# A fused backward kernel: tiles 4 and 5 of the opening each with a square root of its own and a place of its own on TensorE, tile 1 turned two products later

## The chip, the cores and the metric

The kernel runs on one core of one Trainium2 chip. The metric is the time of one execution on the device in microseconds (us). Lower is better. All times below are of one core; "TensorE" multiplies matrices, "VectorE" and "ScalarE" work on elements, "GpSimd" (POOL) and "SyncE" (SP) mostly issue transfers.

## The reference

The reference computes a forward pass and the gradients of nine of its inputs. `x` is `A_q`, 2048 rows of 1024 (bf16).

```python
def _layernorm(x, axis=-1, eps=1e-5):
    m = jnp.mean(x, axis=axis, keepdims=True)
    v = jnp.var(x, axis=axis, keepdims=True)
    return (x - m) / jnp.sqrt(v + eps)
...
    def _B_ref(x, W_gate, W_up, W_down):
        gate = jnp.einsum("bsd,df->bsf", x, W_gate)
        up = jnp.einsum("bsd,df->bsf", x, W_up)
        gate = gate * (lambda x, dt: x.astype(dt))(gate > 0, gate.dtype)
        h = gate * up
        return jnp.einsum("bsf,fd->bsd", h, W_down)
    x = A_q
    xn = _layernorm(x, axis=-1)
    return x + _A_ref(xn, A_k, A_v, A_shift_k, A_ssm_k, A_ssm_D) + _B_ref(xn, B_W_gate, B_W_up, B_W_down)
...
    _out, _vjp = jax.vjp(_f, A_q, A_k, A_v, A_shift_k, A_ssm_k, A_ssm_D, B_W_gate, B_W_up, B_W_down)
    _grads = _vjp(grad_out)
```

`_A_ref` is a long convolution along the rows, done with Fourier transforms; `_B_ref` is a gated layer with 3584 hidden columns. What the change touches is the layer norm of the first six tiles of 128 rows and the first products with `W_gate`, `W_up` and `W_down`.

## The kernel before

The 2048 rows are 16 tiles of 128. The program has a first phase (`hidden`, L1188) that computes the layer norm, gate, up and the gradient of the hidden layer; then the weight gradients (`ps_d`, `ps_w`), the output and the gradient of `x`. `hidden` goes through 14 stages: two halves of 8 tiles, and in each half seven blocks of 512 hidden columns. In a stage each tile has three rows of work on TensorE, each of eight products of 128x128 by 128x512: a gate row (`ps_g`, with `wg`), an up row (`ps_u`, with `wu`) and a gradient row (`ps_h`, from the turned gradient `goT` and the turned `W_down`, `wdT`). The convolution's work is interleaved from later stages on.

Stage 0 is the opening: nothing is there yet, and the layer norm, the loads and the products run against each other. The order on TensorE is written out by hand (`keep_in_program_order`), and so is most of that on VectorE and ScalarE.

- `ln_load` (L941) loads tiles 0 to 3 one by one, tiles 4 and 5 as one chunk in two transfers (the second one is `ln_rest`, L955), and then chunks of two tiles (`LN_CHUNKS`). Chunk 5 holds tiles 6 and 7.
- `layer_norm` (L958) is a generator; each `next(ln)` issues the next part. For a tile it takes the mean (on ScalarE a pass that sums, `sums`, L968; on VectorE `bn_stats`), subtracts it (`moved`, L1008), takes the sum of squares on ScalarE, then a root: `variance` (L1011) and `root` (L982) add epsilon on VectorE and take the square root on ScalarE, `inverse` (L987) refines and inverts it on VectorE. Tiles 0 to 2 are turned and multiplied with the mean off but unscaled (`bare`), and scaled later by `rstd`; from tile 3 on a tile is scaled (`scale`, L997) before it is turned. `kept` (L1029) scales a copy of tiles 0 to 2 for the store of `xn`.
- `flip_xn` (L1152) turns a tile on TensorE: eight 128x128 products with the identity into a PSUM bank (`pst_x`), then copies into `xnT` on VectorE (on ScalarE for tile 4). Tiles 6 and 7 are turned by DMA.
- `first_rows` (L1278) is the order of the first rows: gate rows of tiles 0 and 1 pair by pair of products, up rows likewise, then gate and up of tiles 2 and 3, with functions called in the middle (`second_tile`, `third_tile`, `last_mid`). `flip(k)` turns all tiles below `k` that aren't turned. In `up`, `mid` is called after four products, `after={k: f}` behind product k, counted from 0.
- `grad` (L1417) does gradient rows in pairs; in row 1 it calls `flip_ahead` (L1388) after four products, which turns tiles 4 and 5 one after the other. Then `gate_up(4)` does gate rows 4 and 5, up rows 4 and 5; `grad(2)` and `grad(4)` follow with gradient rows 2 to 5.
- Before anything else `warm` (L1173) issues 40 products of zeros, 128 wide, while the first tile is loaded.
- Products of a stage store `h` and `ug` through POOL's queue; loads go through SP's queue, in the order in which they are issued there.

The wait for a value is on the engine's own queue: each engine works through its instructions in order, and one that waits holds those behind it.

Of the kernel before, what the change touches and what calls it, by code (L numbers as in the profile page):

```python
# [14 lines left out]
ALU = mybir.AluOpType  # L15
# [864 lines left out]
class LnMlp:  # L880
# [77 lines left out]
    def layer_norm(self, xn_d, jpool, jtag, spool):  # L958
# [5 lines left out]
        def act(out, in_, func, **kw):  # L964
            self.ln_act = nc.scalar.activation(out=out, in_=in_, func=func, **kw)
            return self.ln_act

        def sums(out, x, func, **kw):  # L968
            jk = jpool.tile([P, D], BF16, name="ln_j", tag=jtag)
            return act(jk[:, 0:x.shape[-1]], x, func, accum_out=out, **kw)  # L970
# [50 lines left out]
        def half_mean(x, s, b, k):  # L1021
            part = spool.tile([P, 2, 6], F32, name="ln_bn")
            hold(V.bn_stats(out=part[:, 0], in_=x[:, 0:h]))
            hold(sums(s[:, 0, k:k + 1], x[:, h:D], ACT.Copy, scale=-1.0 / D))
            hold(V.tensor_tensor(out=s[:, 1, k:k + 1], in0=part[:, 0, 1:2], in1=part[:, 0, 4:5], op=ALU.add))
            hold(V.scalar_tensor_tensor(out=b[:, 0, k:k + 1], in0=s[:, 1, k:k + 1], scalar=-0.25, in1=s[:, 0, k:k + 1],
                                        op0=ALU.mult, op1=ALU.add))

        def kept(out, c, st):  # L1029
            hold(V.tensor_scalar(out=out, in0=c, scalar1=self.rstd[:, st:st + 1], scalar2=None, op0=ALU.mult))  # L1030
            self.kept.append(lambda: nc.gpsimd.dma_start(out=xn_d[st * P:(st + 1) * P, :], in_=out))
# [19 lines left out]
            hold(V.bn_stats(out=bn[:, k], in_=x2[:, k * h:k * h + h]))  # L1051
        hold(V.bn_aggr(out=b2[:, 0:2, 0], in_=bn[:].rearrange("p h s -> p (h s)")))
        hold(moved(c2, x2, b2[:, 0, 0:1], ALU.subtract))
        half_mean(x3, s2, b2, 1)
        hold(sums(s2[:, 2, 1:2], x3, ACT.Square, bias=b2[:, 0, 1:2]))
        self.xn.append(c2)
        yield
        self.pri.now()
        kept(n0, c0, 0)
        hold(V.tensor_scalar(out=b2[:, 1, 1:2], in0=s2[:, 2, 1:2], scalar1=1.0 / D, scalar2=None, op0=ALU.mult))  # L1060
        root(s2, b2, 2, hold)
        hold(moved(x3, x3, b2[:, 0, 1:2]))
# [1 line left out]
        hold(scale(x3, 3))  # L1064
        done(x3, 3)
        yield
        kept(n1, c1, 1)
        kept(n2, c2, 2)
        yield
        st0 = 4  # L1070
        for i, n in list(enumerate(self.LN_CHUNKS))[4:]:
            xt = self.ln_x[i]
            self.pri.now()
            sm, smb = small()
            if i == 4:
                for j in range(n):
                    hold(sums(sm[:, 0, j:j + 1], xt[:, j, :], ACT.Copy, scale=-1.0 / D))
                    hold(act(smb[:, 0, j:j + 1], sm[:, 0, j:j + 1], ACT.Copy))
                    hold(sums(sm[:, 2, j:j + 1], xt[:, j, :], ACT.Square, bias=smb[:, 0, j:j + 1]))
                    moved(xt[:, n + j, :], xt[:, j, :], smb[:, 0, j:j + 1])  # L1080
                    yield
            else:
                for j in range(n):
                    ins = sums(sm[:, 0, j:j + 1], xt[:, j, :], ACT.Copy)
                    if j == 0:
                        hold(ins)
                V.tensor_scalar(out=smb[:, 0, 0:n], in0=sm[:, 0, 0:n], scalar1=-1.0 / D, scalar2=None, op0=ALU.mult)
                for j in range(n):
                    sums(sm[:, 2, j:j + 1], xt[:, j, :], ACT.Square, bias=smb[:, 0, j:j + 1])
                    moved(xt[:, n + j, :], xt[:, j, :], smb[:, 0, j:j + 1])  # L1090
                yield
            variance(sm, smb, n, free)
            root(sm, smb, n, free)
            yield
            inverse(sm, smb, n, st0, free)
            self.pri.now()
            for j in range(n):
                scale(xt[:, n + j, :], st0 + j)
                done(xt[:, n + j, :], st0 + j)
            st0 += n  # L1100
            yield
# [50 lines left out]
    def flip_xn(self, st):  # L1152
        xT = self.act_tile("xnT", st)
        if st > 5:
            self.turned = self.nc.sync.dma_start_transpose(out=xT[:].rearrange("p (a b) -> p a b", b=P),
                                                           in_=self.xn[st])
            return xT
        k1 = 0
        for h in {0: (2, 2, 4), 1: (4, 4)}.get(st, (8,)):
            k0, k1 = k1, k1 + h  # L1160
            pst = self.ps.tile([P, self.DT, P], BF16, name="pst_x", tag="bps")
            for kt in range(k0, k0 + h):
                self.pri.pin(self.nc.tensor.transpose(pst[:, kt, :], self.xn[st][:, kt * P:(kt + 1) * P],
                                                      self.ident[:]), always=True)
            c = 4 if st in (2, 3) else h
            for k in range(k0, k0 + h, c):
                copy = self.nc.scalar.copy if st == 4 else self.nc.vector.tensor_copy
                self.copied = copy(out=xT[:, k * P:(k + c) * P], in_=pst[:, k:k + c, :].rearrange("p a b -> p (a b)"))
                if st < 5:
                    self.tc.keep_in_program_order(self.copied)  # L1170
        return xT
# [16 lines left out]
    def hidden(self, first, goT, load, ln, tables, Wg, Wu, Wd, g, xn_d, h_d, ug_d):  # L1188
# [6 lines left out]
        for n in range(N):  # L1195
# [82 lines left out]
            def first_rows():  # L1278

                held = []  # L1280

                def pair(name, w, seq, after):
                    banks = [self.ps_tile(name) for _ in range(2)]
                    for i, (s, q) in enumerate(seq):
                        for kt in (2 * q, 2 * q + 1):
                            self.pri.pin(nc.tensor.matmul(banks[s][:], lhsT=xT[s][:, kt * P:(kt + 1) * P], rhs=w(kt),
                                                          start=(kt == 0), stop=(kt == self.DT - 1)), always=True)
                        if i in after:
                            after[i]()
                    return banks  # L1290

                def second_tile():
                    flip(2)
                    next(ln)

                def third_tile():
                    flip(3)
                    next(ln)
                    flag(0)
                    flag(1)  # L1300

                def last_mid():
                    flip(4)
                    for f in held:
                        f()
                    next(ln)
                    chunk(1)
                ps = pair("ps_g", wg, ((0, 0), (0, 1), (0, 2), (1, 0), (1, 1), (1, 2), (0, 3), (1, 3)), {0: second_tile})
                for s in range(2):
                    gate(s, True, ps=ps[s])  # L1310
                    yield from step()
                next(ln)
                ps = pair("ps_u", wu, [(s, q) for q in range(4) for s in range(2)], {5: third_tile})
                for s in range(2):
                    up(s, None, {}, lambda *fs: held.extend(fs), True, ps[s])
                    yield from step()
                gate(2, True)
                yield from step()
                up(2, None, {3: last_mid})
                chunk(1)  # L1320
                yield from step()
                gate(3, True)
                chunk(1)
                yield from step()
                up(3, hold=True)
                chunk(1)
                yield from step()

            def gate_up(sp):
                end = sp == HS - 2  # L1330
                if ahead:
                    flip(sp + 2)
                for s in (sp, sp + 1):
                    gate(s)
                    yield from step(self.PACE[0])
                if end:
                    (load_up if ahead else load_gate)()
                for s in (sp, sp + 1):
                    up(s)
                    yield from step(self.PACE[1])  # L1340
                if end and ahead:
                    for q in range(4):
                        load_down(q)
                elif end:
                    load_up()
                if swap:
                    next_rows(sp)
# [38 lines left out]
                    next_grads(sp + 2)  # L1386

            def flip_ahead(sp):  # L1388
                flip(min(sp + 6, HS))
                if sp == 0:  # L1390
                    with self.tc.issue_after(self.copied.ins):
                        chunk()

# [33 lines left out]
                        next(ln)  # L1427

            if ahead:
                self.warm(40)  # L1430
                next(ln)
                flip(1)
                next(ln)
                yield from first_rows()
# [516 lines left out]
```

## Time and profile before

| what | us |
|---|---|
| runs of the kernel | 1857.24, 1853.23, 1857.38 |
| their median | 1857.24 |
| the profiled execution, its own time | 1854.18 |
| its span in the profile | 1852.0 |
| TensorE busy in the span | 1843.9 |
| VectorE, ScalarE busy | 1119.3, 646.3 |

The profile is of one execution. PE is TensorE's products, PEld its weight loads, DVE VectorE, ACT ScalarE, POOL GpSimd, SP SyncE; a "q" behind the name means the sequencer of that engine, which issues transfers. A row of a timeline has the start in us from the start of the span, the length, engine, line of the source, operation, what it writes and reads, how many of them, and in brackets how long the engine had been idle and what ended that. Successive instructions of an engine can overlap in such rows, since a row ends when the last result is written. L10xx and L11xx are lines of the kernel before; in the changed kernel the same code stands nine lines further down in the layer norm's last part and in `flip_xn`, and nine to seventeen further in `hidden`.

### The profile page before, as it was taken

How to read it: one execution, taken by the hardware profiler on the slowest of the kernel's cores; microseconds unless marked ns; L12 is line 12 of the kernel's file. 1: busy time of each engine (PE TensorE's matmuls, PEld its weight loads, DVE VectorE, ACT ScalarE, POOL GpSimd, SP SyncE). 2: the span in 40 equal slices, each digit the busy share in tenths (PEclk: the TensorE clock that was granted, in tenths of full speed). 3: DMA queues.
4: the chain of work that ended last, by engine and by line, in shares of the span. 5: the costliest groups of instructions: out<-in, count | busy, mean ns of one | idle time of the engine just before them, and what ended most of it. 6: DMA issues, size and time to landing. Idle time of an engine off the chain costs nothing.

```text
span 1852.0 us, 32391 instructions
## 1 busy us (share of the span) xinstructions
PE 1843.9 (100%) x13184; PEld 848.3 (46%) x13184; DVE 1119.3 (60%) x1651; ACT 646.3 (35%) x1212; POOL 34.9 (2%) x72
## 2 busy tenths in 40 slices
PE   9999999999999999999999999999999999999999
PEld 4444444444444444444444444444444544444444
DVE  6656798698789758485685677821212222566652
ACT  5644544444454454545544554330000000111100
POOL 1200000000000000000000000000000000000000
PEclk9999999999999999999999999999999999999999
DMA  9996669968767866639567445379999867799973
GB/s 240 285 241 168 154 163 233 218 172 199 186 158 193 250 156 169 160 105 270 136 149 179 140 119 158 108 229 248 261 232 255 182 145 170 172 210 216 204 152 74
DMA packets 746822, 345.18 MB, mean 186 GB/s; under 512 B 578105, under 2 KB 715313, under 8 KB 746673
## 3 DMA queue, kind: packets, MB, share of 16 engines
q1 hardware_dynamic: 732880, 311.39, 70.7%
q10 hardware_dynamic: 9632, 17.04, 3.0%
q0 software_dynamic: 4160, 14.68, 2.4%
q8 instruction: 103, 1.69, 0.4%
q14 instruction: 47, 0.38, 0.1%
HBM read 143.79 MB, written 103.83 MB: 134 GB/s over the span
## 4 chain that ended last, share of the span: by engine, by line
PE 96%; DVE 1%; SPq 1%; DMA 1%; issue 0%; ACT 0%; DVEq 0%
PE ps_x L1800 21%; PE ps_w L1503 20%; PE ps_o L1668 10%; PE ps_g L1119 10%; PE ps_u L1119 10%; PE ps_h L1119 10%; PE ps_d L1503 9%; PE ps_c L83 4%; PE ps_d L1519 2%; SPq L1137 0%; PE ps_r L1702 0%; PE ps_w L1519 0%; DMA xn_nat<-xn_d 0%; DVE arena L343 0%; DMA wg<-in_B_W_gate_dram 0%
## 5 line engine op out<-in xcount | busy, mean ns | idle before, releaser
L1503 PE MATMUL ps_w<-ugs,xn_nat 128*128 128x512 bf16 x1728 | 381.1, 379 | 0.0
L87 ACT CAST arena<-ps_c 128x512 bf16<-128x512 f32 x576 | 293.8, 611 | 104.1 <-PE ps_c L83 103.9
L1119 PEld LDWEIGHTS <-xnT 128*128 128x128 bf16 x1760 | 169.1, 98 | 204.8 <-issue 5.0
L1503 PEld LDWEIGHTS <-xn_nat 128*128 128x128 bf16 x1728 | 165.4, 98 | 200.7 <-issue 6.1
L343 DVE STREAM_TRANSPOSE arena<-arena 128x1024 f32<-128x1024 f32 x96 | 179.4, 1932 | 112.6 <-ACT arena L87 102.1
L1119 PE MATMUL ps_h<-wdT,goT 128*128 128x512 bf16 x896 | 203.5, 379 | 0.0
L1119 PE MATMUL ps_u<-wu,xnT 128*128 128x512 bf16 x880 | 201.9, 379 | 0.0
L1119 PE MATMUL ps_g<-wg,xnT 128*128 128x512 bf16 x880 | 201.3, 379 | 0.0
L1800 PE MATMUL ps_x<-wgT,ggT 128*128 128x512 bf16 x896 | 198.6, 379 | 0.0
L1800 PE MATMUL ps_x<-wuT,guT 128*128 128x512 bf16 x896 | 198.6, 379 | 0.0
L1818 ACT ACTIVATE w<-xn,m 128x512 f32<-128x512 bf16 x32 | 24.3, 807 | 482.1 <-DVE m L1811 368.8
L1668 PE MATMUL ps_o<-wd,hT 128*128 128x512 bf16 (+1 forms) x896 | 187.6, 372 | 0.0
L1503 PE MATMUL ps_d<-g_nat,hs 128*128 128x512 bf16 x768 | 169.9, 379 | 0.0
L1800 PEld LDWEIGHTS <-guT 128*128 128x128 bf16 x896 | 87.7, 98 | 105.7
L1800 PEld LDWEIGHTS <-ggT 128*128 128x128 bf16 x896 | 87.7, 98 | 105.5
L1119 PEld LDWEIGHTS <-goT 128*128 128x128 bf16 x896 | 86.7, 98 | 104.2 <-issue 1.0
L1668 PEld LDWEIGHTS <-hT 128*128 128x128 bf16 x896 | 87.7, 98 | 100.0
L1398 ACT CAST gh<-ps_h 128x512 bf16<-128x512 f32 x112 | 66.3, 592 | 189.8 <-PE ps_h L1119 182.8
L1506 ACT CAST wi<-ps_w 128x512 bf16<-128x512 f32 x108 | 64.5, 598 | 187.9 <-PE ps_w L1503 152.0
L1660 DVE TENSOR_TENSOR ya<-ya,xe 128x1024 bf16<-128x1024 bf16 x16 | 11.1, 692 | 178.0 <-DMA xe<-xn_d 178.0
L91 DVE TENSOR_TENSOR t<-arena 128x2048 bf16<-128x2048 bf16 x96 | 113.8, 1218 | 0.4
L1503 PEld LDWEIGHTS <-hs 128*128 128x128 bf16 x768 | 73.3, 98 | 88.3 <-issue 1.8
(151 smaller groups left out, 1427.7 us busy)
## 6 DMA issues: line engine op xcount, KB each, us to landing
ugs<-ug_d SPq DMA_DIRECT2D x112, 256.0 KB, 4.6
ug_d<-ru SPq DMA_DIRECT2D x104, 256.0 KB, 3.0
wu<-in_B_W_up_dram SPq DMA_DIRECT2D x56, 256.0 KB, 4.5
hs<-h_d SPq DMA_DIRECT2D x56, 256.0 KB, 5.0
out_dram<-wi SPq DMA_DIRECT2D x56, 256.0 KB, 4.7
wg<-in_B_W_gate_dram SPq DMA_DIRECT2D x55, 256.0 KB, 5.0
h_d<-ht SPq DMA_DIRECT2D x104, 128.0 KB, 2.4
gt<-in_grad_out_dram SPq DMA_DIRECT2D x32, 256.0 KB, 5.5
```

What stands on the lines that cost most here:

```text
L83: self.pri.pin(self.nc.tensor.matmul(out, lhsT=lhsT, rhs=rhs, start=start, stop=stop))
L87: self.pri.pin(self.nc.scalar.copy(out=out, in_=in_))
L91: self.pri.pin(self.nc.vector.tensor_tensor(out=out, in0=in0, in1=in1, op=op))
L343: self.pri.pin(self.nc.vector.transpose(out=df[:, c0:c0 + 32, :], in_=sf[:, c0:c0 + 32, :]))
L1119: self.pri.pin(self.nc.tensor.matmul(ps[:], lhsT=xT[:, kt * P:(kt + 1) * P], rhs=w(kt), start=(kt == 0), stop=(kt == self.DT - 1)), always ...
L1398: self.pri.pin(nc.scalar.copy(out=gh[:], in_=ps[:]))
L1503: self.pri.pin(self.nc.tensor.matmul(ps[:], lhsT=lhsT(st), rhs=rhs(st), start=(st == 0), stop=(st == self.ST - 1)))
L1506: self.pri.pin(self.nc.scalar.copy(out=out, in_=ps[:]))
L1519: self.pri.pin(self.nc.tensor.matmul(ps[i][:], lhsT=lhsT(i, st), rhs=rhs(i, st), start=(st == 0), stop=(st == self.ST - 1)))
L1668: nc.tensor.matmul(ps, lhsT=hT[:, kt, :], rhs=self.wd[:, kt, oc], start=(kt == 0), stop=(kt == self.FT - 1))
L1800: nc.tensor.matmul(ps, lhsT=T[:, kt, :], rhs=W[:, kt, oc], start=(i == 0), stop=(i == n - 1))
L1818: nc.scalar.activation(out=w[:, oc], in_=xn[:, oc], func=ACT.Identity, scale=m[:, 7:8], bias=m[:, 6:7])
```

## The change

- `warm` issues 38 products in place of 40.
- Tile 1 is turned behind the second pair of gate products of tile 0 and not behind the first (`{1: second_tile}`).
- Tile 3's mean is taken by one pass over the whole tile on ScalarE; before, VectorE and ScalarE took half a tile each (`half_mean`). The scaled copy of tile 0 is made one part earlier.
- Tile 3 is turned behind five products of up row 2 (`{4: last_mid}`); before, behind four.
- Tiles 4 and 5 have a mean, a root and a scaling each. Before, both shared one root of two columns, and both were scaled behind it.
- Tile 4 is turned in the middle of gradient row 1. Tile 5 is turned in up row 4 behind five products. The order of rows 4 and 5 becomes gate 4, up 4, gate 5, up 5; it was gate 4, gate 5, up 4, up 5.
- All copies of tiles 2 to 5 out of PSUM are made in two halves (`c = 4 if st > 1`).

The compiled program's order differs from the one before only in the opening. On SP, the load of tiles 6 and 7 and two turned loads of the gradient stand ahead of the shift table and the first gate weights of stage 1. On POOL, tile 4's `xn` is stored among the first four tiles, and tile 2's among the next four.

```diff
@@ layer_norm
-        half_mean(x3, s2, b2, 1)
+        hold(sums(s2[:, 0, 1:2], x3, ACT.Copy, scale=-1.0 / D))
+        hold(act(b2[:, 0, 1:2], s2[:, 0, 1:2], ACT.Copy))
+        kept(n0, c0, 0)
         hold(sums(s2[:, 2, 1:2], x3, ACT.Square, bias=b2[:, 0, 1:2]))
         self.xn.append(c2)
         yield
         self.pri.now()
-        kept(n0, c0, 0)
...
-        kept(n1, c1, 1)
-        kept(n2, c2, 2)
-        yield
-        st0 = 4
-        for i, n in list(enumerate(self.LN_CHUNKS))[4:]:
+        for j in range(2):
+            x, c = self.ln_x[4][:, j, :], self.ln_x[4][:, 2 + j, :]
+            sm, smb = small()
+            hold(sums(sm[:, 0, 0:1], x, ACT.Copy, scale=-1.0 / D))
+            hold(act(smb[:, 0, 0:1], sm[:, 0, 0:1], ACT.Copy))
+            hold(sums(sm[:, 2, 0:1], x, ACT.Square, bias=smb[:, 0, 0:1]))
+            hold(moved(c, x, smb[:, 0, 0:1]))
+            if j:
+                yield
+            variance(sm, smb, 1, hold)
+            root(sm, smb, 1, hold)
+            inverse(sm, smb, 1, 4 + j, held)
+            hold(scale(c, 4 + j))
+            done(c, 4 + j)
+            yield
+            if j == 0:
+                kept(n1, c1, 1)
+                kept(n2, c2, 2)
+                yield
+        st0 = 6
+        for i, n in list(enumerate(self.LN_CHUNKS))[5:]:
...
@@ flip_xn
-            c = 4 if st in (2, 3) else h
+            c = 4 if st > 1 else h
@@ first_rows
                 def last_mid():
                     flip(4)
-                    for f in held:
+                    for f in held[0:3]:
                         f()
                     next(ln)
-                    chunk(1)
-                ps = pair("ps_g", wg, ((0, 0), (0, 1), (0, 2), (1, 0), (1, 1), (1, 2), (0, 3), (1, 3)), {0: second_tile})
+                    held[3]()
+                ps = pair("ps_g", wg, ((0, 0), (0, 1), (0, 2), (1, 0), (1, 1), (1, 2), (0, 3), (1, 3)), {1: second_tile})
...
-                up(2, None, {3: last_mid})
-                chunk(1)
+                up(2, None, {4: last_mid}, hold=True)
+                next(ln)
                 yield from step()
                 gate(3, True)
-                chunk(1)
                 yield from step()
                 up(3, hold=True)
-                chunk(1)
+                next(ln)
@@ gate_up
-                if ahead:
-                    flip(sp + 2)
+                if ahead and not end:
+                    gate(sp)
+                    yield from step(self.PACE[0])
+                    up(sp, None, {4: lambda: flip(sp + 2)})
+                    yield from step(self.PACE[1])
+                    gate(sp + 1)
+                    yield from step(self.PACE[0])
+                    up(sp + 1)
+                    yield from step(self.PACE[1])
+                    return
@@ flip_ahead
-                flip(min(sp + 6, HS))
+                flip(min(sp + (6 if sp else 5), HS))
                 if sp == 0:
+                    next(ln)
                     with self.tc.issue_after(self.copied.ins):
                         chunk()
@@ hidden
-                self.warm(40)
+                self.warm(38)
```

More of the change, by code (lines that the diff above doesn't have):

```diff
@@ L1074, in layer_norm @@
             sm, smb = small()
[L1075 to L1091, printed above, removed]
+            for j in range(n):
+                ins = sums(sm[:, 0, j:j + 1], xt[:, j, :], ACT.Copy)
+                if j == 0:
+                    hold(ins)
+            V.tensor_scalar(out=smb[:, 0, 0:n], in0=sm[:, 0, 0:n], scalar1=-1.0 / D, scalar2=None, op0=ALU.mult)
+            for j in range(n):
+                sums(sm[:, 2, j:j + 1], xt[:, j, :], ACT.Square, bias=smb[:, 0, j:j + 1])
+                moved(xt[:, n + j, :], xt[:, j, :], smb[:, 0, j:j + 1])
+            yield
             variance(sm, smb, n, free)
```

## The prediction

> **What bounds the kernel now.** I read the page first: which engine is full, and which engine the chain that ended last runs on.
>
> ```profile
> PE 1843.9 (100%) x13184; PEld 848.3 (46%) x13184; DVE 1119.3 (60%) x1651; ACT 646.3 (35%) x1212; POOL 34.9 (2%) x72
> PE 96%; DVE 1%; SPq 1%; DMA 1%; issue 0%; ACT 0%; DVEq 0%
> ```
>
> TensorE is busy for 1843.9 of 1852.0 us and carries 96% of the chain. An edit that leaves its products as they are can only win from the 8 us in which it isn't busy, so the second view is what it waited for, over the whole span (total, times, longest).
>
> ```profile
> PE pst_x L1163 <- DVE ln_x L998: 2.5, 1, 2.5
> PE ps_warm L1179 <- DVE warm L1176: 1.0, 1, 1.0
> PE ps_c L83 <- DVE ru L1258: 0.6, 1, 0.6
> PE pst_x L1163 <- DVE ln_x L1009: 0.5, 1, 0.5
> ```
>
> The change aims at the first row (tiles 4 and 5 are turned together and wait for their scaling) and the last (tile 1 is turned before its mean is taken off). The second is the start itself, the third lies far behind the opening. The third view is the timeline of TensorE in the opening: start, length, what, and in brackets the idle time before it.
>
> ```profile
> 1.02 4.45 PE L1179 MATMUL ps_warm<-warm 128*128 128x128 bf16 x40 [1.02 <-DVE warm L1176]
> 5.26 0.99 PE L1163 MATMUL pst_x<-ident,ln_x 128*128 128x128 bf16 x8
> 6.09 0.59 PE L1286 MATMUL ps_g<-wg,xnT 128*128 128x512 bf16 x2
> 7.17 0.62 PE L1163 MATMUL pst_x<-ident,ln_x 128*128 128x128 bf16 x8 [0.48 <-DVE ln_x L1009]
> 7.63 3.18 PE L1286 MATMUL ps_g<-wg,xnT 128*128 128x512 bf16 x14
> 17.14 0.62 PE L1163 MATMUL pst_x<-ident,ln_x 128*128 128x128 bf16 x8
> 21.91 2.75 PE L1119 MATMUL ps_h<-wdT,goT 128*128 128x512 bf16 x12
> 27.19 1.27 PE L1163 MATMUL pst_x<-ident,ln_x 128*128 128x128 bf16 x16 [2.52 <-DVE ln_x L998]
> 28.29 1.03 PE L1119 MATMUL ps_h<-wdT,goT 128*128 128x512 bf16 x4
> 32.61 3.62 PE L1119 MATMUL ps_u<-wu,xnT 128*128 128x512 bf16 x16
> 36.06 7.07 PE L1119 MATMUL ps_h<-wdT,goT 128*128 128x512 bf16 x32
> ```
>
> Lengths overlap, so I count from start to start: sixteen products take 36.06 - 32.61 = 3.45 us, 0.216 each; eight turns take 7.63 - 7.17 = 0.46. Counted so, the first two gate products end at 6.52 and TensorE stands 0.65 until 7.17; the twelve gradient products end at 24.50 and it stands 2.69 until 27.19; the sixteen turns take 1.10 where 0.92 would do, 0.18 more. From 28.29 on rows follow each other without a gap. So all that can be won is about 3.5 us, and the point to compare is the start of gradient row 2: 36.06 now. The matmuls behind it are the same in both kernels, so what is won there stays.
>
> **Tile 1 two products later.** TensorE now does the second pair of gate products of tile 0 before turning tile 1.
>
> ```profile
> 6.64 0.48 DVE L1009 TENSOR_SCALAR ln_x<-ln_x,ln_b 128x1024 bf16<-128x1024 bf16 x1
> 6.70 0.37 SPq L1111 DMA_DIRECT2D wu<-in_B_W_up_dram  x1
> ```
>
> The pair needs the second piece of gate weights. The load at 6.70 was held on the queue until that piece had landed, so it is there at 6.7. The pair runs 6.70 to 7.13, tile 1 is subtracted at 7.12 and turned at 7.17 as before, and two products are already done: 0.43 won, 0 if the piece comes 0.4 later.
>
> **Two warm-up products fewer.** By their 0.106 us each (4.24 from 1.02 to 5.26 for forty) TensorE is free 0.21 earlier.
>
> ```profile
> 4.75 0.61 DVE L1009 TENSOR_SCALAR ln_x<-ln_x,ln_b 128x512 bf16<-128x512 bf16 x2
> ```
>
> The first half of tile 0 is only subtracted near 5.1, so the turn still starts near 5.2: I take 0, between 0.1 won and the clock rival below.
>
> **Tile 4 in gradient row 1, tile 5 in up row 4.** TensorE reaches tile 4 at 24.50 - 0.43 = 24.07. Tile 4 now has a root of its own and doesn't wait for tile 5. What it and tile 5 cost on VectorE, the in-order queue that decides, comes from these rows.
>
> ```profile
> 16.01 0.16 DVE L993 TENSOR_TENSOR ln_s<-ln_s 128x2 f32<-128x2 f32 x1
> 16.20 0.16 DVE L994 TENSOR_TENSOR ln_b<-ln_s 128x2 bf16<-128x2 f32 x1
> 16.60 0.49 DVE L998 TENSOR_SCALAR ln_x<-ln_x,rstd 128x1024 bf16<-128x1024 bf16 x1
> 17.80 0.76 DVE L1168 COPY xnT<-pst_x 128x512 bf16<-128x512 bf16 x2 [0.31 <-PE pst_x L1163]
> 18.47 0.74 DVE L1255 SCALAR_TENSOR_TENSOR ru<-ps_u,rstd,ru 128x512 bf16<-128x512 f32 x1
> 19.13 0.48 DVE L1009 TENSOR_SCALAR ln_x<-ln_x,ln_b 128x1024 bf16<-128x1024 bf16 x1
> 20.52 0.28 DVE L1243 TENSOR_SCALAR ru<-ru 128x512 bf16<-128x512 bf16 x1
> 20.72 0.41 DVE L1264 TENSOR_TENSOR ht<-ru 128x512 bf16<-128x512 bf16 x1
> 21.06 0.87 DVE L1030 TENSOR_SCALAR ln_x<-ln_x,rstd 128x1024 bf16<-128x1024 bf16 x2
> 25.85 0.68 DVE L1399 TENSOR_TENSOR ru<-ru,gh 128x1024 bf16<-128x1024 bf16 x1
> 30.97 0.17 DVE L1087 TENSOR_SCALAR ln_b<-ln_s 128x2 bf16<-128x2 f32 x1 [1.79 <-ACT ln_j L965]
> 31.18 0.88 DVE L1009 TENSOR_SCALAR ln_x<-ln_x,ln_b 128x1024 bf16<-128x1024 bf16 x2
> ```
>
> Tile 3 is turned at 17.14 - 0.43 + 0.22 (one up product more stands ahead of it) = 16.93; its copies follow 0.66 later, as from 17.14 to 17.80, and end at 18.35. The compiled order of the new kernel then has, up to the scaling of tile 5: four masked products (4 x 0.74), four products (4 x 0.42), two subtractions (2 x 0.48), a flag 0.28, the scaling of tiles 1 and 2 (0.87), two gradient products (2 x 0.68), the scaling of tile 4 (0.49) and two chains of six short instructions at 0.2 from start to start (12 x 0.2). That is 11.0. Neighbours that don't depend on each other overlap by 0.09 (19.13 with 0.48 in length, and the next row, one with no part in this, stood at 19.52); at eleven such pairs 1.0 goes, and 10.0 is left. The list starts at 18.3. Tile 4 is scaled some 3.8 us into it, at 22.1, two us before TensorE wants it: the 2.69 is gone. Tile 5 is scaled from 28.3 to 28.8.
>
> TensorE comes to tile 5 at 24.07 + 0.46 (turn) + 0.86 (four products) + 1.73 (gate row 4) + 1.08 (five of up row 4) = 28.2. It waits 0.6 there. That is the smaller half of what is late next. ScalarE:
>
> ```profile
> 21.33 1.06 ACT L965 ACTIVATE ln_j<-ln_x 128x1024 bf16<-128x1024 bf16 x1 [1.44 <-DMA ln_x<-in_A_q_dram]
> 23.90 0.58 ACT L1240 ACTIVATE ru<-ps_g 128x512 bf16<-128x512 f32 x1
> 27.84 1.01 ACT L1168 COPY xnT<-pst_x 128x1024 bf16<-128x1024 bf16 x1 [2.73 <-PE pst_x L1163]
> 28.75 1.06 ACT L965 ACTIVATE ln_j<-ln_x 128x1024 bf16<-128x1024 bf16 x1
> 30.75 0.19 ACT L965 ACTIVATION_READ_ACCUMULATOR ln_j<-ln_x 128x1 f32 x1
> ```
>
> In ScalarE's new order tile 5's root stands ahead of the sums of tiles 6 and 7. The root needs tile 5's variance plus epsilon, which VectorE has 8.5 us into the ten (behind it only four short instructions and the second gradient product, 1.4), at 26.8; the root ends near 27.05. The sums take 30.94 - 28.75 = 2.2 and end at 29.3. In VectorE's new order the mean of tiles 6 and 7 (L1087, now L1096) and their two subtractions stand **ahead of tile 5's copies**; they stood behind them. So the copies wait for ScalarE: 29.3 + 0.2 + 0.88 = 30.4, the first half is copied at 30.8, and gate row 5 starts at 30.85 instead of 29.9. It and up row 5 take 3.45, and gradient row 2 starts at 34.3. Against 36.06 that is **1.75 us won**. The same by waits: 0.43 + 2.69 + 0.18 go, 0.6 and 0.95 come.
>
> The first root and ScalarE's two copies of tile 4 need no price: tile 5's rows land at 21.3 (that load ended the idle time of the first row), its sums and square end at 23.9 (second row), then comes a cast, and half of the 1.01 copy follows the turn at 25.3; gate row 4 wants it at 25.4. With that cover gone it waits a few tenths, but behind it tile 5 waits less by as much. Tile 3's mean moves wholly to ScalarE: half a pass more there (0.5, by the 1.06 of a whole one), three instructions fewer on VectorE. Its scaling ends at 17.09 now; if it stayed there the turn at 16.93 would wait 0.2. I take 0, as VectorE's share falls by more than ScalarE's grows. Tile 0's kept copy only moves ahead of tile 2's copies, which wait for TensorE anyway.
>
> On SP the shift table and the first two gate loads of the next stage fall behind the load of tiles 6 and 7 and the next two turned loads of the gradient.
>
> ```profile
> 19.62 0.58 SPq L237 DMA_DIRECT2D sk_b<-in_A_shift_k_dram  x1
> 21.90 0.37 SPq L951 DMA_DIRECT2D ln_x<-in_A_q_dram  x1
> ```
>
> So the load of tiles 6 and 7 goes out near 19.6, not 21.9, and gradient rows 2 and 3 get theirs 2.3 earlier, more than TensorE is ahead. The gate weights of stage 1 have a whole stage of cover. On POOL, tile 4's store takes tile 2's place among the four early ones; only loads for tiles 8 to 15 hang on these buffers. Both: nothing.
>
> **The rivals.** *The new waits don't come* (0.15). If VectorE gets through its list by 1.5 us sooner, or the trace's overlaps are larger than I count, the 0.6 and 0.95 vanish: 3.3 won, 1853.9. For it: before, VectorE still found idle gaps of 0.2 to 0.5 here. Against: the two queue positions are fixed in the program.
>
> *The clock* (0.08). Up to 5.26 a 128-wide product takes 0.106, at 7.17 it takes 0.0575: the fast pace comes after some 4.1 us of work. Two fewer leave TensorE idle for 0.1 to 0.2 near 5.1. Were the change of pace put off by as long again, 4.1 us of work at 0.46 loss each would cost 1.9, less the 0.2 it stands for the weights; VectorE's list starts later by as much, and the 1.75 is used up: 1857.2. Against: 0.2 idle in four is little. The Trainium skill, "TensorE: Matmul & The Clock Gate", Part 1 (The HAM clock gate), says that the pace changes after about 3.4 us in a window that runs freely, not after a count of matmuls; here 4.1 passed, which that allows. By that rule trimming two matmuls changes nothing, unless the idle bit falls into the deciding window.
>
> *Slower: tiles 6 and 7 land late* (0.07). Their sums now stand ahead of tile 5's copies, so their load, hidden before, is on the path. It decides from 27.1 on; each us later is one us on TensorE, the gain is gone at 28.85, and at 31.0 the time is 2.1 over before, 1859.4. For it: the load shares the DMA engines with the turned loads. Against: it goes out 2.3 earlier, and before its reader ran at 28.75 without a wait.
>
> *The change doesn't do what it says* is excluded for TensorE: the compiled order has all three turns moved.
>
> **How the numbers follow.** The profiled execution took 1854.18 us, 2.18 around a span of 1852.0; less 1.75 it is 1852.4. The runs before gave 1853.23, 1857.24 and 1857.38, so they differ by 4.1 among themselves, more than the change brings; against their median I forecast 1857.24 - 1.75 = 1855.5, with chance 0.62 (0.08 is for none of these). The range goes from 1851.2, near the lowest run less 1.75 to 2, to 1858.2, the highest run with a gain lost and a part of the slow rival. 0.3% is 5.6 us, about what a measurement of this kernel can tell from no change. More than that is won only with 3.3 in the lower group of runs, 0.07; lost only with a load later than 34, or something unlisted, 0.04.
>
> **What would show it.** Right: tile 1 turned with no wait above 0.1 behind four gate products; tile 4 turned near 24 without a wait; a wait for VectorE of about half a us ahead of tile 5's turn near 28.8, and one of about 1 us ahead of gate row 5 for a copy queued behind L1096; gradient row 2 near 34.3. Wrong: no wait at gate row 5; tile 4's turn still waiting; sums of tiles 6 and 7 that wait for a DMA; warm-up pace beyond 6 us; or a new gap behind 36 us.

## The result, and the profile after

The changed kernel takes 1851.78 us in the median of 22 runs (1851.24 to 1854.17), the kernel before 1854.86 in as many (1853.03 to 1857.65). The ratio is 0.9984, with a 95% interval of 0.9978 to 0.9991: about 3 us less, within the 0.3% that the forecast calls no change, and inside its range. The profiled executions took 1851.98 and 1854.18, with spans of 1850.1 and 1852.0.

What TensorE waited for in the changed kernel, over the whole span (total, times, longest):

```profile
PE ps_warm L1188 <- DVE warm L1185: 1.0, 1, 1.0
PE pst_x L1172 <- DVE ln_x L998: 0.8, 1, 0.8
PE ps_c L83 <- DVE ru L1267: 0.6, 1, 0.6
PE ps_g L1128 <- DVE xnT L1177: 0.5, 1, 0.5
PE pst_x L1172 <- DVE ln_x L1009: 0.4, 1, 0.4
```

The 2.5 us ahead of tiles 4 and 5 are gone. 0.8 of the same kind is left, and one row is new: gate row 5 waits 0.5 for a copy (`xnT`) on VectorE. Where they lie, in TensorE's timeline of the changed kernel:

```profile
5.16 0.66 PE L1172 MATMUL pst_x<-ident,ln_x 128*128 128x128 bf16 x8
5.83 1.04 PE L1295 MATMUL ps_g<-wg,xnT 128*128 128x512 bf16 x4
7.28 0.62 PE L1172 MATMUL pst_x<-ident,ln_x 128*128 128x128 bf16 x8 [0.41 <-DVE ln_x L1009]
17.07 0.61 PE L1172 MATMUL pst_x<-ident,ln_x 128*128 128x128 bf16 x8
24.26 0.61 PE L1172 MATMUL pst_x<-ident,ln_x 128*128 128x128 bf16 x8
29.35 0.62 PE L1172 MATMUL pst_x<-ident,ln_x 128*128 128x128 bf16 x8 [0.81 <-DVE ln_x L998]
29.81 0.81 PE L1128 MATMUL ps_u<-wu,xnT 128*128 128x512 bf16 x3
31.10 1.90 PE L1128 MATMUL ps_g<-wg,xnT 128*128 128x512 bf16 x8 [0.49 <-DVE xnT L1177]
34.57 7.07 PE L1128 MATMUL ps_h<-wdT,goT 128*128 128x512 bf16 x32
```

Tile 4 is turned at 24.26 without a wait, tile 5 waits, gate row 5 waits again, and gradient row 2 starts at 34.57 where it started at 36.06: 1.49 us won here. Both waits are read from the queues of VectorE (first three rows) and ScalarE:

```profile
28.63 0.67 DVE L998 TENSOR_SCALAR ln_x<-ln_x,rstd 128x1024 bf16<-128x1024 bf16 x1
29.62 0.17 DVE L1096 TENSOR_SCALAR ln_b<-ln_s 128x2 bf16<-128x2 f32 x1 [0.33 <-ACT ln_j L965]
30.63 0.75 DVE L1177 COPY xnT<-pst_x 128x512 bf16<-128x512 bf16 x2
```

```profile
27.31 0.20 ACT L965 ACTIVATE ln_s<-ln_b 128x1 f32<-128x1 bf16 x1 [0.84 <-DVE ln_b L983]
29.40 0.19 ACT L965 ACTIVATION_READ_ACCUMULATOR ln_j<-ln_x 128x1 f32 x1
```

Tile 5's root runs at 27.31, the sums of tiles 6 and 7 behind it end at 29.59, L1096 waits for them, and tile 5's copies stand behind L1096. Of the rest of the 1.9 us in the span, 0.3 is won early in the second kind of weight gradients, where the kernel before followed a transfer (`xn_nat<-xn_d`); its origin wasn't looked into.

So the profiled executions give 2.2 us and the medians 3.1. The experiments show where the rest most likely is.

### The profile page after: what moved, and what is told of

It reads as the page before. It is cut to its first block, busy times and chain, and to the rows that moved or that the text cites. A ratio compares the mean times of both kernels' runs of the same rounds, so it can differ in the third digit from the quotient of the medians.

```text
span 1850.1 us, 32392 instructions
## 1 busy us (share of the span) xinstructions
PE 1843.3 (100%) x13182; PEld 847.1 (46%) x13182; DVE 1120.7 (61%) x1654; ACT 646.7 (35%) x1215; POOL 34.9 (2%) x72
## 4 chain that ended last, share of the span: by engine, by line
PE 97%; DVE 2%; issue 0%; ACT 0%; DMA 0%; SPq 0%; DVEq 0%
PE ps_x L1817 21%; PE ps_w L1520 20%; PE ps_o L1685 10%; PE ps_g L1128 10%; PE ps_u L1128 10%; PE ps_h L1128 10%; PE ps_d L1520 9%; PE ps_c L83 4%; PE ps_d L1536 2%; PE ps_w L1536 1%; PE ps_r L1719 0%; DVE arena L343 0%; DVE ru L1264 0%; DMA ln_x<-in_A_q_dram 0%; PE ps_u L1295 0%
```

## The experiments

Each experiment ran in one of three sessions, and each session has the kernel before beside it (medians 1855.27, 1855.54 and 1855.48 us); a ratio is against that one. The changed kernel's 1851.78 is from a session of its own, so a difference of a few tenths to it is not clear of noise.

**1 and 2. The two parts alone.** The kernel before with the part at tile 1:

```diff
-(1, 3)), {0: second_tile})
+(1, 3)), {1: second_tile})
-                self.warm(40)
+                self.warm(38)
```

> The kernel before with only the later turn of tile 1 and 38 warm-up products. Theory: in the kernel before, the turn of tiles 4 and 5 hangs on a chain that starts when tile 5's rows land (21.3 us), not on TensorE, so the 0.43 us won at tile 1 only make the wait ahead of tile 4's turn longer by as much: 2.9 to 3.0 instead of 2.5, gradient row 2 still near 36.0, time 0 to 0.1 us under the kernel before. Rival (the waits add up by themselves): gradient row 2 at 35.6, 0.43 us faster.

Measured: 1855.74 us, ratio to the kernel before 1.0001 (0.9993 to 1.0010). Nothing is won, as the theory said. The profile isn't the one expected, though: a wait of 3.79 ahead of tile 4's turn, not 2.9 to 3.0, and gradient row 2 at 38.73, not near 36.0. Experiments 3 to 6 show where that comes from. The changed kernel with the same two lines undone:

> The changed kernel with tile 1 turned where it was before and 40 warm-up products; tiles 4 and 5 as changed. Theory: in the changed kernel the end of the opening hangs on VectorE's list, which starts when tile 3 is turned; tile 3's turn comes some 0.4 us later, so gradient row 2 starts at 34.9 to 35.0 instead of 34.57, and the time is 0.3 to 0.4 us over the changed kernel. Rival (the list has slack): gradient row 2 at 34.57, no difference to the changed kernel.

Measured: 1852.47 us (1852.04 to 1852.76), ratio 0.9983 (0.9974 to 0.9992); gradient row 2 at 34.91 in its profile, 0.34 later than in the changed kernel. So tile 1's part is worth nothing where the next wait hangs on something else, and by the profiles 0.3 us where it doesn't; the ratios (0.9983 and 0.9984) can't tell these two kernels apart. Nearly the whole gain is in tiles 4 and 5.

**3 to 6. When tile 5's rows are loaded.** One line is moved, `late` in both kernels, `early` in both:

```diff
     goT = [b.load_T(g, 0, "goT", 8, True)]
-    b.ln_rest()
     goT.append(b.load_T(g, 1, "goT", 9, True))
+    b.ln_rest()
```

```diff
+    b.ln_rest()
     goT = [b.load_T(g, 0, "goT", 8, True)]
-    b.ln_rest()
     goT.append(b.load_T(g, 1, "goT", 9, True))
```

> The kernel before with the load of tile 5's rows issued behind the second turned load of the gradient, some 1.2 us later. Theory: in the kernel before this landing starts the chain to tile 4's turn, so tiles 4 and 5 are turned at 28.3 to 28.5 instead of 27.19 and the time is 1.1 to 1.3 us over the kernel before; a run in which the rows land late is then a slow run, which would explain why the kernel before spreads more than the changed one. Rival (VectorE's list sets that turn, not the landing): 0 to 0.4 us.

> The kernel before with the load of tile 5's rows issued ahead of the first turned load of the gradient, some 1.3 us earlier. Theory: the landing of these rows varies from run to run, and in the kernel before it starts the chain to the turn of tiles 4 and 5. With the load earlier VectorE's list sets that turn (near 26.5), about 0.6 us under the profile of the kernel before, and the time varies less: the median 1 to 2 us under the kernel before, and its runs within some 2 us. Rival (the spread has another origin): 0.6 us under the kernel before, with the same spread of 4 to 5 us.

> The changed kernel with the load of tile 5's rows issued behind the second turned load of the gradient, some 1.2 us later. Theory: the changed kernel has about 1 us of slack on that landing; the copies of tile 4 come near 26.1 and gate row 4 waits up to 1 us, but tile 5's turn then waits less, and gradient row 2 comes at 34.6 to 34.9: 0 to 0.3 us over the changed kernel. Rival (the landing is on its path): 1.2 us over the changed kernel.

> The changed kernel with the load of tile 5's rows ahead of the first turned load of the gradient. Theory: in the changed kernel the landing is off the path in nearly all runs, so nothing is won in the median: within 0.2 us of the changed kernel. Rival (the landing is still on its path in many runs): 0.5 to 1.3 us under the changed kernel.

| kernel, tile 5's rows | median us | lowest to highest | ratio to the kernel before |
|---|---|---|---|
| before, late | 1857.83 | 1856.80 to 1858.48 | 1.0015 (1.0007 to 1.0024) |
| before, early | 1852.87 | 1852.56 to 1855.09 | 0.9989 (0.9980 to 0.9997) |
| changed, late | 1853.20 | 1851.60 to 1854.24 | 0.9992 (0.9983 to 1.0001) |
| changed, early | 1851.83 | 1851.45 to 1852.70 | 0.9984 (0.9975 to 0.9992) |

In the kernel before, the place of one load is worth 5 us from end to end, and loading it early brings 2.7 us by itself, more than the 1 to 2 expected and most of what the change brings. In the changed kernel loading it early does nothing. Loading it late costs some 1.4 us there, where I had said 0 to 0.3. In its profile (1851.60 us, the fastest of its 11 runs) the rows land at 22.20, gate row 4 waits 0.66 for tile 4's copies, tile 5 then doesn't wait, and gradient row 2 starts at 34.05, so nothing is lost. Three of the other runs had a mean clock of 0.999 and took 1854.1 to 1854.2. The loss probably comes from runs in which the rows land later, but no profile shows one.

The mechanism in the kernel before is exact. These rows give ScalarE's first pass over tile 5, which starts when the rows land, and the turn of tile 4, first for the kernel with tile 1's part alone, then for the one with the late load:

```profile
22.58 1.06 ACT L965 ACTIVATE ln_j<-ln_x 128x1024 bf16<-128x1024 bf16 x1 [2.65 <-DMA ln_x<-in_A_q_dram]
28.44 1.89 PE L1163 MATMUL pst_x<-ident,ln_x 128*128 128x128 bf16 x16 [3.79 <-DVE ln_x L998]
```

```profile
23.04 1.06 ACT L965 ACTIVATE ln_j<-ln_x 128x1024 bf16<-128x1024 bf16 x1 [3.09 <-DMA ln_x<-in_A_q_dram]
28.90 1.27 PE L1163 MATMUL pst_x<-ident,ln_x 128*128 128x128 bf16 x16 [4.17 <-DVE ln_x L998]
```

28.44 - 22.58 = 5.86, 28.90 - 23.04 = 5.86, and in the kernel before 27.19 - 21.33 = 5.86. A landing that comes later moves the turn one to one, whatever TensorE won before it. That is why experiment 1 found a longer wait and no gain. With the early load the distance is another one:

```profile
19.75 1.06 ACT L965 ACTIVATE ln_j<-ln_x 128x1024 bf16<-128x1024 bf16 x1
26.30 1.27 PE L1163 MATMUL pst_x<-ident,ln_x 128*128 128x128 bf16 x16 [1.73 <-DVE ln_x L998]
```

ScalarE no longer waits for the rows, and 6.55 us pass to the turn. There VectorE's list sets the turn, as expected (26.5).

But the late load cost 2.6 us in the median (1857.83 against 1855.27), twice what I expected. In the profiles gradient row 2 comes 3.40 later (39.46 against 36.06), and the turn of tile 4 only 1.71 of that. Experiment 1 has the same surplus, and its windows show why (columns: stretch, its length, busy time and count of TensorE, weight loads, VectorE, ScalarE, POOL, then the granted clock of TensorE, DMA share and GB/s):

```profile
26.00:28.00 2.00, 0.00 (x0) 0.00 (x0) 1.93 (x8) 0.36 (x1) 0.54 (x1) 1.00 1.47 242
28.00:30.00 2.00, 1.56 (x15) 1.57 (x16) 1.03 (x2) 0.49 (x1) 0.70 (x1) 0.60 0.94 187
30.00:32.00 2.00, 1.78 (x8) 0.82 (x7) 0.69 (x1) 2.00 (x4) 0.00 (x0) 0.55 1.04 330
32.00:34.00 2.00, 2.00 (x11) 0.90 (x10) 1.33 (x4) 2.00 (x4) 0.00 (x0) 1.00 1.16 335
```

After the wait of 3.79 the granted clock is 0.60 and 0.55 of full in two stretches: read as half pace, that is 1.6 + 1.8 = 3.4 us of it. From tile 4's turn to gradient row 2 it takes 38.73 - 28.44 = 10.29 us here, against 36.06 - 27.19 = 8.87 in the profile of the kernel before: the drop costs 1.4 us, in the late kernel 1.7 (39.46 - 28.90 = 10.56).

The mean clock of each run hints at how often that happens. One drop takes 1.7 us of full clock, 0.0009 of a run: the two profiles with one drop have a mean clock of 0.999, and the one with two (experiment 8 below) has 0.998. The kernel before ran 100 times beside these experiments. In 32 runs the mean clock was 1.000, and they took 1853.8 us in the median; in 68 it was 0.999 or 0.998, and they took 1855.7. The changed kernel had 1.000 in all 22 runs, the early kernel before in 10 of 11, the late one in none. The profile that I forecast from, at 1.000, is of the kind of the 32. That the drop in the 68 stands behind the wait for tile 4 is argued from experiments 1 and 4: the mean clock doesn't say where it fell, and no profile of the kernel before has one. The Trainium skill, "TensorE: Matmul & The Clock Gate", Part 1 (The HAM clock gate), has this as a rule: idle windows of about 3.4 us, which run freely, bring the pace down to half until a busy one. The 3.4 us at half pace agree. That the same wait meets the window differently from run to run would explain why the kernel before falls on both sides, and so would a landing that varies; no run here shows the window itself.

**7 and 8. TensorE kept busy in the wait.** To take the clock away and leave the landing, 38 turns of the identity into tile 4's own bank were put ahead of its turn; the first kernel is the one before, the second has the late load as well.

```diff
+            for _ in range(38 if st == 4 else 0):
+                self.pri.pin(self.nc.tensor.transpose(pst[:, 0, :], self.ident[:], self.ident[:]), always=True)
```

> The kernel before with 38 turns of the identity ahead of tile 4's turn (about 2.2 us of TensorE work that nobody reads, inside the wait of 2.5 us and more). Theory: the upper group of runs of the kernel before, at 1855 and over, are those in which the wait grows beyond some 3.4 us, so that the granted clock falls and the next 4 us of products run at half pace. With TensorE kept busy the wait that is left is 0.4 to 2 us and the clock stays: every run at a mean clock of 1.000, the upper group gone, median 1853.5 to 1854.5, some 1 us under the kernel before. Rival (the late landing alone makes the spread): the same times as the kernel before, median near 1855.4 and runs up to 1857.

> The kernel before with tile 5's rows loaded later and the same 38 turns of the identity ahead of tile 4's turn. Theory: without them this load order gave 1857.83 us in the median, with the clock down in every run; with them only the later landing is left (1.3 to 1.9 us over the lower group of the kernel before): 1855.2 to 1856.3 us, clock 1.000 in nearly all runs. Rival: 1857.8 as before.

Measured: 1856.38 and 1858.10 us, ratios 1.0008 (0.9999 to 1.0017) and 1.0017 (1.0008 to 1.0025). The times missed what was expected. The opening of the first did what it should: a wait of 0.45, no drop, gradient row 2 at 36.21, and 7 of 11 runs at a clock of 1.000 where the kernel before had 7 of 33 beside it. But these seven took 1855.7 us in the median and not 1853.6: in their profiles both kernels then lost more in stage 1, at a gradient row whose turned `W_down` came late. The first:

```profile
63.79 2.32 PE L1119 MATMUL ps_h<-wdT,goT 128*128 128x512 bf16 x10 [1.95 <-DMA wdT<-in_B_W_down_dram]
```

SyncE had issued the four loads of that kind from 48.92 to 59.65 us, in the kernel before from 48.78 to 57.80. Why it took longer isn't settled. In the second the clock still fell, after a wait of 2.37 us only, and once more after the late `W_down`, behind a wait of 2.64:

```profile
29.23 1.27 PE L1165 MATMUL pst_x<-ident,ln_x 128*128 128x128 bf16 x16 [2.37 <-DVE ln_x L998]
30.00:32.00 2.00, 2.00 (x13) 1.02 (x12) 0.69 (x1) 2.00 (x4) 0.00 (x0) 0.64 1.11 378
32.00:34.00 2.00, 2.00 (x7) 0.65 (x5) 0.95 (x3) 2.00 (x4) 0.00 (x0) 0.51 1.16 335
68.06 4.00 PE L1119 MATMUL ps_h<-wdT,goT 128*128 128x512 bf16 x10 [2.64 <-DMA wdT<-in_B_W_down_dram]
68.00:70.00 2.00, 1.94 (x5) 0.69 (x5) 0.27 (x1) 0.59 (x1) 0.00 (x0) 0.53 1.21 362
70.00:72.00 2.00, 2.00 (x7) 0.78 (x6) 0.42 (x1) 0.00 (x0) 0.00 (x0) 0.62 1.04 283
```

So "beyond some 3.4 us", as I had put it, is wrong: an idle stretch of 2.4 or 2.6 us can do it. Ahead of the first stood turns of the identity, and one could doubt that they count as work; around the second stand ordinary products. Both waits are shorter than the window of 3.4 us that the Trainium skill has in the part named above; here the measurement decides.

**9 to 12. The two waits that are left.** First the sums, mean and subtractions of tiles 6 and 7 behind tile 5's turn; then, besides, gradient row 2 between up row 4 and gate row 5.

```diff
-                    up(sp, None, {4: lambda: flip(sp + 2)})
+                    def fifth():
+                        flip(sp + 2)
+                        with self.tc.issue_after(self.copied.ins):
+                            chunk()
+                    up(sp, None, {4: fifth})
...
-                    with self.tc.issue_after(self.copied.ins):
-                        chunk()
```

> The changed kernel with the sums, mean and subtractions of tiles 6 and 7 issued behind the turn of tile 5, so that VectorE has tile 5's copies ahead of them. Theory: the wait ahead of tile 5's turn stays (0.8 us), the one ahead of gate row 5 (0.5) goes; gradient row 2 near 33.9 instead of 34.57, 0.5 to 0.65 us under the changed kernel. Rival: tiles 6 and 7 are ready later, and gate row 6 waits for their turning by as much: no difference, or slower.

```diff
+                    up(sp)
                     yield from step(self.PACE[1])
+                    def fifth():
...
+                    yield from grad_row(2, {3: fifth})
...
                 for s in (sp, sp + 1):
+                    if ahead and s == 2:
+                        continue
```

> As the kernel with the mean of tiles 6 and 7 later, and gradient row 2 done between up row 4 and gate row 5, with tile 5 turned in its middle. Theory: TensorE comes to tile 5 about 1.7 us later in its order and finds it scaled, and its copies done before gate row 5: both waits go, 1.3 to 1.6 us under the changed kernel. Rival: gate row 6 comes so early that tiles 6 and 7, turned by transfer, aren't there, and a new wait ahead of it takes the gain back.

Measured: 1852.18 us (1851.12 to 1855.96) and 1853.80 (1851.67 to 1859.49), ratios 0.9985 (0.9976 to 0.9993) and 0.9996 (0.9987 to 1.0005). Both openings did what the theory said. In the first, gate row 5 starts without a wait, and gradient row 2 comes at 33.80:

```profile
29.20 0.62 PE L1172 MATMUL pst_x<-ident,ln_x 128*128 128x128 bf16 x8 [0.81 <-DVE ln_x L998]
30.34 1.90 PE L1128 MATMUL ps_g<-wg,xnT 128*128 128x512 bf16 x8
33.80 7.07 PE L1128 MATMUL ps_h<-wdT,goT 128*128 128x512 bf16 x31
```

In the second there is no wait at tile 5 either. But the rival was right on the time. In the second, gate row 6 waits for tiles turned by transfer:

```profile
41.66 3.63 PE L1128 MATMUL ps_g<-wg,xnT 128*128 128x512 bf16 x16 [1.87 <-DMA xnT<-ln_x]
```

A transfer is on the path again, and the runs spread over 8 us. In the first, gate rows 6 and 7 take 0.24 us more than sixteen products need in its profile (1851.41); the median shows nothing of the 0.77 won, and its slowest run, 1855.96, is the only one with a mean clock below 1.000.

The last two leave that margin alone and take work out of VectorE's list, first the scaled copies of tiles 1 and 2 (0.88 us), and then, besides, put tile 5's copies ahead of L1096 with the sums where they were.

```diff
             if j == 0:
-                kept(n1, c1, 1)
-                kept(n2, c2, 2)
                 yield
...
+        def kept_late():
+            kept(n1, c1, 1)
+            kept(n2, c2, 2)
+            k = self.kept
+            self.kept = k[:2] + k[-2:] + k[2:-2]
...
+                    def fifth():
+                        flip(sp + 2)
+                        self.kept_late()
+                    up(sp, None, {4: fifth})
```

> The changed kernel with the scaled copies of tiles 1 and 2 (0.87 us of VectorE) moved behind tile 5's copies, and stored in the order of the kernel before. Theory: VectorE's list up to tile 5 sets the end of the opening, so tile 5 is scaled 0.85 us earlier, its turn waits 0 to 0.2 us, the sums of tiles 6 and 7 and so gate row 5 come 0.85 us earlier: gradient row 2 near 33.7, time 0.8 to 0.9 us under the changed kernel. Rival (another queue is next): less than 0.3 us.

```diff
-                if j == 0:
+                if j == 0 or i == 5:
...
+            if i == 5:
+                yield
-            V.tensor_scalar(out=smb[:, 0, 0:n], in0=sm[:, 0, 0:n], scalar1=-1.0 / D, scalar2=None, op0=ALU.mult)
+            mean = V.tensor_scalar(out=smb[:, 0, 0:n], in0=sm[:, 0, 0:n], scalar1=-1.0 / D, scalar2=None, op0=ALU.mult)
+            if i == 5:
+                hold(mean)
...
                         flip(sp + 2)
+                        self.tc.keep_in_program_order(self.copied)
+                        chunk()
                         self.kept_late()
...
-                    with self.tc.issue_after(self.copied.ins):
-                        chunk()
+                    next(ln)
```

> As the kernel with the scaled copies later, and VectorE has tile 5's copies ahead of the mean of tiles 6 and 7, while ScalarE takes the sums of these tiles as early as in the changed kernel. Theory: both waits of the opening go, gradient row 2 near 33.1, and tiles 6 and 7 are scaled about when they are in the changed kernel (34.7), just in time for gate row 6: 1.3 to 1.5 us under the changed kernel. Rival: gate row 6 waits for the transfer that turns tile 6, which varies from run to run, and the time spreads as that of the kernel with gradient row 2 between: no better than the changed kernel.

Measured: 1850.95 us (1850.56 to 1851.82), ratio 0.9978 (0.9969 to 0.9987), and 1851.63 (1850.82 to 1853.76), ratio 0.9981 (0.9972 to 0.9990). The first, in TensorE's timeline:

```profile
28.59 0.62 PE L1176 MATMUL pst_x<-ident,ln_x 128*128 128x128 bf16 x8
30.34 1.90 PE L1132 MATMUL ps_g<-wg,xnT 128*128 128x512 bf16 x8 [0.48 <-DVE xnT L1181]
33.80 7.07 PE L1132 MATMUL ps_h<-wdT,goT 128*128 128x512 bf16 x32
```

Tile 5's wait is gone, gradient row 2 comes 0.77 earlier, and the time is 0.83 under that of the changed kernel (ratios 0.9978 and 0.9984, from different sessions), as expected: VectorE's list set the end of the opening, as the prediction had it. This is the best version measured, with its runs within 1.3 us. The second has neither wait and gradient row 2 at 33.03. It was expected 1.3 to 1.5 us under the changed kernel and isn't clear of it, since it pays again for tiles 6 and 7:

```profile
42.48 1.90 PE L1136 MATMUL ps_g<-wg,xnT 128*128 128x512 bf16 x8 [0.64 <-DMA xnT<-ln_x]
```

## Why the prediction was right, and where its size was off

- *Tile 1, 0.43 won.* The two products went ahead, but tile 1 was turned later, at 7.28 and not at 7.17, and a wait of 0.41 stayed that I had put at 0.1 or less. At the start of the up rows of tiles 0 and 1, 0.28 was won (10.37 against 10.65).
- *Two warm-up products, nothing.* Tile 0 was turned at 5.16, 0.10 earlier, the gain I had named as the upper end. The clock rival, at this place, didn't come.
- *Tile 4 near 24 without a wait.* 24.26, none. The few tenths ahead of gate row 4 didn't come either: it starts at 25.57, right behind the gradient products.
- *VectorE's list of 10.0 us.* From 18.39 to tile 5's scaling at 28.63 it took 10.24.
- *Waits of 0.6 and 0.95.* By starts 0.97 (tile 5 wanted at 28.38) and 0.64 (gate row 5 at 30.46). The sum is 1.61 against 1.55, its parts are the other way round; the causes are as predicted. Experiment 11 shows that of the first by taking 0.88 us out of the list. Experiment 9 shows that of the second by moving L1096 behind the copies.
- *Gradient row 2 at 34.3, 1.75 won.* 34.57, 1.49 won.
- *Tiles 6 and 7 late.* Not in this kernel. Experiments 10 (gradient row 2 between) and 12 (copies first) show that the margin is small: TensorE came to gate row 6 1.8 and 1.5 us earlier than in the changed kernel, and waited 1.87 and 0.64 for these tiles.

What was mis-sized is the term that goes. I took the wait of 2.69 as a constant of the kernel before, and said that the matmuls behind it are the same. It is a sample: its end is set by the landing of tile 5's rows, which came at 21.33, 21.47 and 22.58 us in the three profiles that have this load in this place, and behind a longer wait the granted clock fell, for 1.4 to 1.7 us. In two runs of three the mean clock shows a drop somewhere. Among the runs with a clock of 1.000 the gain is 1853.8 - 1851.8 = 2.0 (the two from different sessions), near the 2.2 of the two profiles; among all it is 3.1. The clock rival was thought of at the warm-up, where it does nothing, and not at the longest wait of the kernel.

The time itself was forecast 3.7 us too high, and it lies only 0.6 above the lower end of a range of 7 us. Two errors with the same sign add up to that: the median of three runs, 1857.24, lies 2.4 over that of 22, and the gain was 1.3 larger than forecast. So the range held because it was wide. By its size alone the gain of 3.1 would speak for the rival of 3.3, in which the new waits don't come; the rows show that they came, with nearly the sum that the forecast gave them.

## What to carry to other kernels

A wait whose end hangs on a transfer's landing can be worth more than its length in one profile: read who started the chain, check that the distance to its end is constant over profiles (5.86 us here in all those in which ScalarE waited for the rows), and look at the mean clock of single runs for what the wait does to the products behind it. Then try the cheap edit first: the early load alone brought 2.7 of the 3.1 us. After each gain ask which landing now has the smallest margin: what experiments 10 and 12 won in the opening was lost again, in part or whole, when a transfer came onto the path.

## What the runs showed of the hardware that wasn't expected

- The granted clock of TensorE fell to half for 3.4 us after waits of 3.79, 4.17, 2.37 and 2.64 us, and not after 2.52 (the profile of the kernel before; 2.69 by starts) or 1.95. A wait need not be as long as the time at half pace, and the length of the wait alone doesn't decide.
- The granted clock on record doesn't show the slow start. It reads 1.00 from the first us on, while the first 40 products take 0.106 us each, against 0.0575 for each of the eight turns at 7.17. So a mean clock of 1.000 says only that it didn't drop later.
- One load of 256 KB, issued one place earlier or one place later in a queue, moves the median of an execution by 5 us of 1855 between the two: 1852.87 and 1857.83.
